# A modelled SBUF port in the kernel's own scheduler, ELU sums on VectorE, and a longer look-ahead

## The chip, the cores and the metric

One core of a Trainium2 chip runs the whole program. The metric is the device time in microseconds of one execution; the median of three runs of the kernel before is 866.75 us. The engines are TensorE (PE in the profile, its weight loads PEld), VectorE (DVE), ScalarE (ACT), GpSimd (POOL) and SyncE (SP), which here issues nearly all DMAs from one in-order queue.

## The reference

Local attention with two kinds of mask, followed by an ELU feed-forward layer, all in float32:

```python
# q, k, v: (8, 8, 576, 64); w_in: (512, 2048); w_out: (2048, 512)
scores = (q @ k.transpose(0, 1, 3, 2)) / sqrt(64)
rel = pos[:, None] - pos[None, :]
mask_plain = (rel >= 0) & (rel < 32)                          # heads 0 to 3
mask_dil = (rel >= 0) & (rel < 128) & (rel % 4 == 0)          # heads 4 to 7
scores = where(mask, scores, -1e9)
attn = exp(scores - scores.max(-1)); attn /= attn.sum(-1) + 1e-9
x = (attn @ v), heads side by side                            # (4608, 512)
h = x @ w_in
g = where(h > 0, h, exp(min(h, 0)) - 1)
out = g @ w_out                                               # (4608, 512)
```

## The kernel before

The 4608 tokens are nine chunks of 512. The first three ("plain chunks", c = 0, 1, 2) are computed directly: for each of 16 blocks f of the hidden dimension, a first product into a PSUM bank `h`, an ELU (ScalarE exp and relu, VectorE `stt!`), a split of the result into a rounded high part and a remainder ("cast" on ScalarE, "rest" on VectorE, since three single-pass products of high and low parts replace one float32 product), and a second product into `o_ps` for block f - 2. The other six chunks are taken two at a time as three "wide" chunks (`wide_chunk`, w = 0, 1, 2), with a Strassen-like scheme of seven products instead of eight in both matrix products: 28 "in" steps and 28 "out" steps of 12 matmuls each. Their weight combinations (names like S1, A22) are computed once on chip from the weights, stored in DRAM (`combined`, `plain_out`, `sums_out`) and loaded again into a ring of four places (`load_combined`, L950 to L965): the load for step i + 3 can go out when step i - 1 has freed its place. Each "in" step is followed by additions and ELU pieces on VectorE and ScalarE (`behind_inner`). Each "out" step needs an operand "unit" (`make_unit`, L1162): the difference of two ELU blocks (`summed`, for four of the seven names), a cast on ScalarE, a rest on VectorE. At the turn from "in" to "out", units are prepared up to LEAD = 4 ahead in the first wide chunk and up to 7 in the others (L1182). When all four steps of an output are done, `stored` adds two PSUM banks to a copy (`gh`, `x` or `e`, VectorE) and stores to `out_t`; the first of these outputs is C11, written from `gh`.

Attention of the batches b = 2 to 7 runs as side work between these steps, pair of heads by pair: scores on TensorE into the banks `a_ps`, masks added by VectorE into a tile `sm`, then `pair_steps` ("max", "less", "exp", "sum", "more", "over", "times", six copies "placed" into `pt`, and a transpose "turned"), then the product with v. Further side work is the sums of weights for the Strassen scheme ("sums", POOL) and the splits of some weights ("late").

The order of instructions on each engine is fixed by the program's order (`inorder`). That order comes from a small scheduler in the kernel itself: `clock` holds a modelled time for each engine, `Ordered` wraps an engine and advances its clock by a linear cost, `work(until)` emits the side steps that start earliest by these clocks until they would end after `until`, `better` may move a step named in SHARED from its engine to POOL, and `freer` gives a step to VectorE or POOL, whichever ends first by the model. `output_ready` and `scores_ready` decide when TensorE takes a piece of attention. An `Ordered` VectorE writes a tensor_tensor as a scalar_tensor_tensor (L611), except where it reads PSUM (`from_bank`). L614 is the line through which nearly all ordered steps of VectorE, ScalarE and POOL pass, and L607 that of the additions from PSUM; L147 is that of all matmuls.

Of the kernel before, what the change touches and what calls it, by code (L numbers as in the profile page):

```python
# [71 lines left out]
STORE_LAG = 1  # L72
FILL = 3.5
WIDE_STEP = 4.0
# [20 lines left out]
def body(ctx: ExitStack, tc: tile.TileContext, q, k, v, masks, w_in, w_out, out, out_t):  # L95
# [240 lines left out]
    def start_sum(half):  # L336
# [205 lines left out]
    def masks_added(hp, places, sm, eng=nc.vector):  # L542

        dil = hp >= NPAIR // 2
        for i in range(max(len(p) for p in places)):
            for h in range(2):
                n0, n1, s_ps = places[h][i]
                add = eng.from_bank if isinstance(eng, Ordered) else eng.tensor_tensor
                last = add(out=sm[:, h * NU + n0:h * NU + n1, :].rearrange("p n j -> p (n j)"), in0=s_ps[:QB, :(n1 - n0) * 2 * G],
                                        in1=mask_sb[:, int(dil), n0 * 2 * G:n1 * 2 * G], op=ALU.add)  # L550
        return last
# [24 lines left out]
    def probabilities(b, hp, sm, nmx, sums):  # L576
# [13 lines left out]
        return b, hp, tr  # L590

    class Ordered:

# [5 lines left out]

        def cost(self, kw, name=None):  # L600
            if self.name == "POOL" and name in ("copy", "tensor_copy"):
# [3 lines left out]
        def from_bank(self, **kw):  # L605
            clock[self.name] = self.free() + self.cost(kw)
            return inorder(self.eng.tensor_tensor(**kw))  # L607

        def __getattr__(self, name):
            def emit(**kw):  # L610
                if self.name == "DVE" and name == "tensor_tensor":  # L611
                    return self.scalar_tensor_tensor(out=kw["out"], in0=kw["in0"], scalar=1.0, in1=kw["in1"], op0=ALU.mult, op1=kw["op"])
                clock[self.name] = self.free() + self.cost(kw, name)
                return inorder(getattr(self.eng, name)(**kw))  # L614
            return emit

    vec, act, pool = Ordered(nc.vector, "DVE", 0.155, 0.00104), Ordered(nc.scalar, "ACT", 0.19, 0.00083), Ordered(nc.gpsimd, "POOL", 0.45, 0.00185)
# [6 lines left out]
    finished, at = {}, {}  # L624
    phase, late_until, second_done = [0], [2], {}

    def emit_next(pair):

        name, eng, op, kw, *more = better(pair.pop(0), finished.get(id(pair), 0.0))
        clock[eng.name] = max(eng.free(), finished.get(id(pair), 0.0), floor(name))  # L630
        ins = getattr(eng, op)(**(kw() if callable(kw) else kw))
        finished[id(pair)] = clock[eng.name] + LATENCY
# [11 lines left out]
    def better(step, since):  # L644

        name, eng, op, kw, *more = step
        if name[0] not in SHARED or not phase[0] < SHARED_UNTIL:
            return step
        other = [name, pool, {"copy": "tensor_copy"}.get(op, op), kw, *more]
        return min(step, other, key=lambda x: max(x[1].free(), since) + cost(x))  # L650

    def work(until):

        while True:
            side[:] = [pair for pair in side if pair]
            starts = []
            for n, pair in enumerate(side):
                key = pair[0][0]
                if ready_for(key):
                    step = better(pair[0], finished.get(id(pair), 0.0))  # L660
                    start = max(step[1].free(), finished.get(id(pair), 0.0), floor(key))
                    if start + cost(step) <= until:
                        starts.append((start, 0 if key[0][-1] == "!" else 1 if key[0][:4] == "late" else 3 if key[0] == "sums" else 2, n))
            if not starts:
                return
            emit_next(side[min(starts)[-1]])
# [27 lines left out]

    sms, kept = [], []

    def other_sm(*at):
        del sms[1:]
        if at:
            sms.append([at[0].rearrange("p o t -> p (o t)")[:QB, :2 * NU * 2 * G].rearrange("p (u j) -> p u j", u=2 * NU), None])  # L700

    def own_steps(c, f, h_ps):
# [35 lines left out]

    def pair_steps(b, hp, sm):
# [5 lines left out]
        yield ("max", b, hp), vec, "tensor_reduce", dict(out=mx, in_=sm, op=ALU.max, axis=mybir.AxisListType.X)  # L745
        yield ("less", b, hp), vec, "tensor_tensor", dict(out=sm, in0=sm, in1=wide(mx), op=ALU.subtract)
        yield ("exp", b, hp), act, "activation", dict(out=sm, in_=sm, func=AF.Exp, scale=0.125)
# [17 lines left out]
    def one_scores(b, hp):  # L765
# [3 lines left out]
        i = b * NPAIR + hp  # L769
        scores(s_ps, *qk_of.pop(i), True)  # L770
        clock["now"] = clock["PE"]
        room = free_sms()[0]
        sm, room[1] = room[0], (b, hp)
        masks_added(hp, [[(0, NU, a)] for a in s_ps], sm, vec)
        banks_free[0] = clock["DVE"] + LATENCY
        side.append([list(x) for x in pair_steps(b, hp, sm)])
        kept_lists.append(side[-1])
        finished[id(side[-1])] = clock["DVE"]
        load_qk(i + 2)
        landed["qk", i + 2] = clock["PE"] + LANDING  # L780

    def one_output(b, hp):
# [11 lines left out]
        if (b, hp) == (CS + 1, NPAIR - 1):  # L794
            kept.append(sms[-1][0])
            other_sm(slots("a-1'", 0, 1))
        load_v(i + 2)
        landed["v", i + 2] = clock["PE"] + LANDING

    def output_ready():  # L800
# [4 lines left out]
        if phase[0] < HOME[b]:  # L805
            return False
        return max(at["turned", b, hp] + LATENCY, landed.get(("v", b * NPAIR + hp), 0.0), banks_free[0]) <= clock["PE"] + (TOLERANCE if phase[0] > 2 else EARLY)

    def scores_ready():
# [7 lines left out]
        last = ("placed", *rooms[0][1], GU - 1, 1) if rooms[0][1] else None  # L817
        return max(at.get(last, 0.0), landed.get(("qk", b * NPAIR + hp), 0.0), banks_free[0]) <= clock["PE"] + (TOLERANCE if phase[0] > 2 else EARLY)

# [181 lines left out]
    def wide_operand(w, what):  # L1001
# [7 lines left out]
        if do == "make":  # L1009
            for r0, r1, (left, right) in wide_stretches(w, 0, 1):  # L1010
                x0, x1 = {"T1": lambda: (right(0), left(0)), "T2": lambda: (right(1), temporary(w, "T1")[:, :, r0:r1]), "T3": lambda: (right(1), right(0)),
                          "T4": lambda: (left(1), temporary(w, "T2")[:, :, r0:r1])}[name]()
                freer(t[:, :, r0:r1]).tensor_tensor(out=t[:, :, r0:r1], in0=x0, in1=x1, op=ALU.subtract)
        elif t is not None:
# [11 lines left out]
    def wide_chunk(w):  # L1026
# [52 lines left out]
        def added(to, tos, key):  # L1079
            for i in range(2):  # L1080
                vec.from_bank(out=to[i], in0=tos[i], in1=us[key][i], op=ALU.add)

# [70 lines left out]
        def summed(k):  # L1153

            if k < len(over):
# [29 lines left out]
        def stored(name, tos, key):  # L1185

            for r in range(2):
# [3 lines left out]
                for i in range(n):  # L1191
                    cols = slice(i * TC // n, (i + 1) * TC // n)
                    vec.from_bank(out=o[:, cols], in0=tos[r][:, cols], in1=us[key][r][:, cols], op=ALU.add)
                    def write(o=o, t=t, s=s, cols=cols):
# [380 lines left out]
```

## Time and profile before

| | us |
|---|---|
| median of 3 runs (lowest, highest) | 866.75 (865.43, 866.88) |
| the profiled execution | 864.79 |
| its span, first to last instruction | 863.0 |
| TensorE busy | 825.8 |
| VectorE busy | 650.9 |
| ScalarE busy | 519.7 |
| POOL busy | 286.9 |

The mean granted TensorE clock is 0.988. The "busy" of TensorE includes matmuls that run slowly; the rows of a single group (n matmuls in so many us) tell the pace. Rows of the timeline give the start, the length, the engine, the line, the operation, output<-inputs, the shape and the count; in brackets stand the idle time of the engine before the row and what ended it. The time of a VectorE or POOL row runs from its issue to its end, so that it includes time in which it is held up.

### The profile page before, as it was taken

The numbers are of one execution on the slowest core, as the hardware profiler recorded it, in microseconds if no ns is written. First come the engines' busy times: TensorE is split into PE (matmuls) and PEld (weight loads), VectorE is DVE, ScalarE is ACT, GpSimd is POOL, SyncE is SP. The second block draws the span as 40 slices with busy tenths as digits, with TensorE's granted clock in tenths as the row PEclk, the third lists the DMA queues.
The fourth block names the chain that finished last, engine by engine and source line by source line (L and its number), as shares of the span: only waits on it lengthen the run. The fifth ranks groups of instructions, "written<-read, shape, count | busy, mean of one in ns | idle before, by whom it ended". The sixth has DMA issues, their size and how long they took to land.

```text
span 863.0 us, 16083 instructions
## 1 busy us (share of the span) xinstructions
PE 825.8 (96%) x6304; PEld 651.5 (75%) x6304; DVE 650.9 (75%) x758; ACT 519.7 (60%) x873; POOL 286.9 (33%) x250
## 2 busy tenths in 40 slices
PE   6999999999999999899998899999996999999798
PEld 4566888778878778678776678788885888888686
DVE  6999996987757758478979895577799654467972
ACT  5889776665555546668855353688753436676340
POOL 3000001464676666686651722002062020023400
PEclk9999999999999999999999999999998999999999
DMA  8999878646465894899876659766644686666555
GB/s 302 379 384 372 258 225 278 196 159 197 132 216 184 247 283 139 319 373 335 290 254 181 210 169 311 226 181 189 186 154 156 194 264 194 194 193 194 165 178 168
DMA packets 105322, 199.13 MB, mean 231 GB/s; under 512 B 13120, under 2 KB 58528, under 8 KB 104992
## 3 DMA queue, kind: packets, MB, share of 16 engines
q1 hardware_dynamic: 105104, 197.81, 70.8%
q8 instruction: 49, 0.80, 0.4%
q10 hardware_dynamic: 144, 0.31, 0.1%
q14 instruction: 25, 0.20, 0.1%
HBM read 148.54 MB, written 49.55 MB: 230 GB/s over the span
## 4 chain that ended last, share of the span: by engine, by line
PE 76%; DVE 12%; DMA 5%; ACT 4%; issue 2%; SPq 0%; DVEq 0%; POOL 0%; ACTq 0%
PE o_ps L147 39%; PE h L147 24%; PE a_ps L147 13%; DVE a L614 5%; DVE r L614 4%; ACT x L614 1%; DMA outputs<-a-1_3413 1%; DMA r<-sums_out 1%; DMA r<-combined 1%; DMA r<-w_in 1%; DMA vt<-v 1%; ACT a L614 1%; DVE a-1_3413 L607 0%; DMA qt<-q 0%; DVE a-1_3413 L614 0%
## 5 line engine op out<-in xcount | busy, mean ns | idle before, releaser
L147 PE MATMUL o_ps<-a,r 128*128 128x512 f32 x792 | 188.7, 392 | 4.6 <-DVE a L614 4.6
L147 PEld LDWEIGHTS o_ps<-a,r 128*128 128x128 f32 x792 | 147.5, 188 | 37.6 <-DVE a L614 5.8
L147 PE MATMUL o_ps<-r,r 128*128 128x512 f32 x432 | 109.7, 405 | 15.7 <-DMA r<-sums_out 11.8
L147 PEld LDWEIGHTS o_ps<-r,r 128*128 128x128 f32 x432 | 84.0, 196 | 36.6 <-issue 12.6
L614 POOL TENSOR_TENSOR a<-a 128x256 f32<-128x256 f32 (+1 forms) x59 | 59.3, 1009 | 126.0 <-DVE r L614 116.6
L147 PE MATMUL h<-a,r 128*128 128x512 f32 x396 | 94.3, 390 | 0.0
L147 PEld LDWEIGHTS h<-a,r 128*128 128x128 f32 x396 | 74.0, 188 | 15.9
L147 PE MATMUL h<-x,r 128*128 128x512 f32 x324 | 79.7, 395 | 0.0
L147 PE MATMUL o_ps<-a,gh 128*128 128x512 f32 x216 | 76.1, 449 | 0.0
L147 PEld LDWEIGHTS h<-x,r 128*128 128x128 f32 x324 | 60.1, 188 | 13.8 <-DVE a L188 0.2
L147 PE MATMUL a_ps<-a,r 128*128 128x512 f32 x252 | 60.2, 391 | 3.0 <-DVE a L614 1.5
L614 ACT ACTIVATE x<-x 128x1024 f32<-128x1024 f32 (+1 forms) x53 | 54.9, 1041 | 8.3 <-POOL x L614 7.6
L147 PEld LDWEIGHTS a_ps<-a,r 128*128 128x128 f32 x252 | 46.9, 188 | 14.7 <-DVE a L614 2.8
L614 DVE SCALAR_TENSOR_TENSOR a<-a,a 128x1024 fp32r<-128x1024 f32 (+2 forms) x32 | 47.6, 1492 | 7.7 <-ACT a L614 7.3
L614 DVE SCALAR_TENSOR_TENSOR a<-r,a 128x1024 fp32r<-128x1024 f32 x30 | 45.7, 1530 | 10.0 <-ACT a L614 10.0
L147 PEld LDWEIGHTS o_ps<-a,gh 128*128 128x128 f32 x216 | 39.7, 188 | 17.8 <-issue 10.5
L614 ACT CAST a<-r 128x1024 fp32r<-128x1024 f32 x30 | 31.3, 1047 | 34.5 <-DVE r L614 27.1
L614 POOL TENSOR_TENSOR sm<-sm,nmx 96x768 f32<-96x768 f32 x4 | 5.9, 1472 | 126.4 <-DMA out<-e 121.1
L614 ACT CAST a<-a 128x1024 fp32r<-128x1024 f32 (+1 forms) x30 | 28.9, 962 | 29.6 <-DVE a L614 18.3
L147 PE MATMUL o_ps<-r,gh 128*128 128x512 f32 x136 | 42.7, 395 | 0.0
L614 ACT COPY e<-o_ps 128x512 f32<-128x512 f32 x44 | 24.8, 587 | 28.2 <-PE o_ps L147 24.8
L614 DVE SCALAR_TENSOR_TENSOR gl<-e,gh 128x512 fp32r<-128x512 f32 x34 | 28.1, 827 | 17.7 <-ACT gh L614 14.0
(235 smaller groups left out, 1662.0 us busy)
## 6 DMA issues: line engine op xcount, KB each, us to landing
r<-combined SPq DMA_DIRECT2D x84, 512.0 KB, 4.5
r<-sums_out SPq DMA_DIRECT2D x48, 512.0 KB, 4.6
r<-plain_out SPq DMA_DIRECT2D x36, 512.0 KB, 4.2
vt<-v SPq DMA_DIRECT2D x30, 384.0 KB, 4.8
kt<-k SPq DMA_DIRECT2D x29, 304.0 KB, 4.7
qt<-q SPq DMA_DIRECT2D x30, 288.0 KB, 4.2
r<-w_in SPq DMA_DIRECT2D x16, 512.0 KB, 6.8
r<-w_out SPq DMA_DIRECT2D x16, 512.0 KB, 7.2
```

The costliest lines, as they stand in the source:

```text
L147: return inorder(nc.tensor.matmul(to, w, x, **kw))
L614: return inorder(getattr(self.eng, name)(**kw))
```

## The change

- `summed` (the ELU block differences of the "out" operands) always goes to VectorE (SUMMED_BY = "vec"); before, `freer` chose VectorE or POOL. The T differences of `wide_operand` still go through `freer` (MADE_BY = "both").
- The modelled clocks get a shared port: `Ordered.start` lets a VectorE or POOL step with two SBUF inputs (LOCKING) begin only after the other engine's modelled step, and a POOL step pushes VectorE's clock on by the overlap. `better` counts a POOL step double (PORT_COST).
- SHARED shrinks to "placed": "less", "times" and "late" are no longer offered to POOL. Consecutive "placed" copies may start together.
- VectorE's tensor_tensor is issued as such, and the "more" step becomes a tensor_scalar.
- Look-ahead: FILL from 3.5 to 5.5 (how far past TensorE side work is emitted in the plain chunks), LEAD from 4 to 6, BACKLOG from 5 to 8 (how far VectorE may be behind when new scores are taken), EARLY from -1 to 0. The modelled costs of POOL steps are changed too.
- Switches that are off (MASKED_BY_PE, EXP_BY_UNIT empty) or set as before (SUMS_BY = "pool") change nothing.

The core of the diff:

```diff
-FILL = 3.5
+FILL = 5.5
-EARLY = -1.0
+EARLY = 0.0
-LEAD = 4
-BACKLOG = 5.0
-SHARED, SHARED_UNTIL = ("placed", "less", "times", "late"), 3.5
+LEAD = 6
+BACKLOG = 8.0
+LOCKING = {"DVE": ("tensor_tensor", "scalar_tensor_tensor", "tensor_scalar", "tensor_copy"), "POOL": ("tensor_tensor", "tensor_copy", "copy")}
+SHARED = ("placed",)
+PORT_COST = 1.0
...
             if self.name == "POOL" and name in ("copy", "tensor_copy"):
-                return 0.3 + 0.0009 * (kw if isinstance(kw, int) else length(kw["out"]))
+                return 0.35 + 0.00053 * (kw if isinstance(kw, int) else length(kw["out"]))
...
+        def start(self, name, kw, since=0.0):
+            t = max(self.free(), since)
+            if self.locks(name, kw):
+                for a, b in port[PORT_WITH[self.name]]:
+                    if a <= t < b:
+                        t = b
+                        if self.name == "POOL":
+                            break
+            return t
...
             def emit(**kw):
-                if self.name == "DVE" and name == "tensor_tensor":
-                    return self.scalar_tensor_tensor(out=kw["out"], in0=kw["in0"], scalar=1.0, in1=kw["in1"], op0=ALU.mult, op1=kw["op"])
-                clock[self.name] = self.free() + self.cost(kw, name)
+                t = self.start(name, kw)
+                clock[self.name] = t + self.cost(kw, name)
+                if self.locks(name, kw):
+                    port[self.name] = port[self.name][-7:] + [(t, clock[self.name])]
+                    if self.name == "POOL":
+                        clock["DVE"] += sum(max(0.0, min(b, clock["POOL"]) - max(a, t)) for a, b in port["DVE"])
...
-    ... pool = ... Ordered(nc.gpsimd, "POOL", 0.45, 0.00185)
+    ... pool = ... Ordered(nc.gpsimd, "POOL", 0.19, 0.00212)
...
-        return min((vec, pool), key=lambda eng: eng.free() + eng.cost(length(out)))
+        return min((vec, pool), key=lambda eng: eng.start("tensor_tensor", 0) + eng.cost(length(out)))
...
-        yield ("more", b, hp), vec, "scalar_tensor_tensor", dict(out=sums, in0=sums, scalar=1e-9, in1=sums, op0=ALU.add, op1=ALU.max)
+        yield ("more", b, hp), vec, "tensor_scalar", dict(out=sums, in0=sums, scalar1=1e-9, scalar2=None, op0=ALU.add)
...
-                    freer(to).tensor_tensor(out=to, in0=x, in1=y, op=ALU.subtract)
+                    (freer(to) if SUMMED_BY == "both" and w == 0 else vec).tensor_tensor(out=to, in0=x, in1=y, op=ALU.subtract)
```

More of the change, by code (lines that the diff above doesn't have):

```diff
@@ L80 @@
 TOLERANCE = 0.0
-EARLY = -1.0
+EARLY = 0.0
 HOME = {2: 1, 3: 2, 4: 2.4, 5: 3.2, 6: 3.2, 7: 4.2}
 START = 1.0
-LEAD = 4
-BACKLOG = 5.0
-SHARED, SHARED_UNTIL = ("placed", "less", "times", "late"), 3.5
-SUMS_FROM = 7
+LEAD = 6
+BACKLOG = 8.0
+LOCKING = {"DVE": ("tensor_tensor", "scalar_tensor_tensor", "tensor_scalar", "tensor_copy"), "POOL": ("tensor_tensor", "tensor_copy", "copy")}
+PORT_WITH = {"DVE": "POOL", "POOL": "DVE"}
+SHARED = ("placed",)
+SHARED_UNTIL = 3.5
+SUMS_FROM = 7
+PORT_COST = 1.0
+SUM_COST = 0.0
+SUM_DELAY = 0.0
+SUMMED_BY = "vec"
+MADE_BY = "both"
+SUMS_BY = "pool"
+MASKED_BY_PE = ()
+EXP_BY_UNIT = ()
 LATE_AT = 2, 4, 5, 7, 9, 11, 12
@@ L363, in start_sum, with banks_after @@
         kept_lists.append(steps)
+    bank_user = [None]
+    def banks_after():
+        return banks_free[0] if not bank_user[0] else at.get(bank_user[0], 1e9) + LATENCY
     x32 = {}
@@ L547, in masks_added @@
                 n0, n1, s_ps = places[h][i]
-                add = eng.from_bank if isinstance(eng, Ordered) else eng.tensor_tensor
-                last = add(out=sm[:, h * NU + n0:h * NU + n1, :].rearrange("p n j -> p (n j)"), in0=s_ps[:QB, :(n1 - n0) * 2 * G],
+                last = eng.tensor_tensor(out=sm[:, h * NU + n0:h * NU + n1, :].rearrange("p n j -> p (n j)"), in0=s_ps[:QB, :(n1 - n0) * 2 * G],
                                         in1=mask_sb[:, int(dil), n0 * 2 * G:n1 * 2 * G], op=ALU.add)
@@ L590, in probabilities @@
         return b, hp, tr
+    port = {"DVE": [], "POOL": []}
     class Ordered:
@@ L600, in cost, with locks @@
         def cost(self, kw, name=None):
+            if self.name == "ACT" and isinstance(kw, dict) and length(kw["out"]) <= 2 * G:
+                return 0.33
             if self.name == "POOL" and name in ("copy", "tensor_copy"):
-                return 0.3 + 0.0009 * (kw if isinstance(kw, int) else length(kw["out"]))
+                return 0.35 + 0.00053 * (kw if isinstance(kw, int) else length(kw["out"]))
             return self.fixed + self.each * (kw if isinstance(kw, int) else max(length(kw[n]) for n in ("out", "in_", "in0") if n in kw))
-        def from_bank(self, **kw):
-            clock[self.name] = self.free() + self.cost(kw)
-            return inorder(self.eng.tensor_tensor(**kw))
+        def locks(self, name, kw):
+            if self.name == "ACT" or name not in LOCKING[self.name]:
+                return False
+            return not isinstance(kw, dict) or all(kw[n].space != bass.MemoryType.PSUM for n in ("in_", "in0", "in1") if n in kw)
@@ L631, in emit_next @@
         ins = getattr(eng, op)(**(kw() if callable(kw) else kw))
-        finished[id(pair)] = clock[eng.name] + LATENCY
+        ends_at[id(pair)] = max(ends_at.get(id(pair), 0.0), clock[eng.name])
+        if not pair or pair[0][0][0] != name[0] or name[0] not in ("exps", "placed"):
+            finished[id(pair)] = ends_at.pop(id(pair)) + LATENCY
         passed.add(name)
@@ L646, in better, with begins @@
         name, eng, op, kw, *more = step
[L647 to L650, printed above, removed]
+        others = []
+        if name[0] in SHARED and phase[0] < SHARED_UNTIL:
+            others.append([name, pool, {"copy": "tensor_copy"}.get(op, op), kw, *more])
+        if name[0] == "sums":
+            other = [name, vec, op, kw, *more] if op == "tensor_tensor" else [name, act, "copy", kw, *more]
+            if SUMS_BY == "vec":
+                return other
+            if SUMS_BY == "both":
+                others.append(other)
+        return min([step, *others], key=lambda x: begins(x, since) + cost(x) * (1 + PORT_COST if x[1] is pool else 1) + (SUM_COST if x[0][0] == "sums" and x[1] is not pool else 0))
+    def begins(step, since):
+        return step[1].start("no lock" if step[0][0] == "stt!" else step[2], step[4] if callable(step[3]) else step[3], since)
     def work(until):
@@ L660, in work @@
                     step = better(pair[0], finished.get(id(pair), 0.0))
-                    start = max(step[1].free(), finished.get(id(pair), 0.0), floor(key))
+                    start = begins(step, max(finished.get(id(pair), 0.0), floor(key)))
                     if start + cost(step) <= until:
-                        starts.append((start, 0 if key[0][-1] == "!" else 1 if key[0][:4] == "late" else 3 if key[0] == "sums" else 2, n))
+                        starts.append((start + (SUM_DELAY if key[0] == "sums" else 0.0), 0 if key[0][-1] == "!" else 1 if key[0][:4] == "late" else 3 if key[0] == "sums" else 2, n))
             if not starts:
@@ L769, in one_scores @@
         i = b * NPAIR + hp
-        scores(s_ps, *qk_of.pop(i), True)
+        if b in MASKED_BY_PE:
+            for a in s_ps:
+                mm(a[:QB, :NU * 2 * G], ones_sb, mask_sb[:, int(hp >= NPAIR // 2), :], start=True, stop=False)
+        scores([a[:QB, :NU * 2 * G] for a in s_ps], *qk_of.pop(i), b not in MASKED_BY_PE)
         clock["now"] = clock["PE"]
@@ L773, in one_scores @@
         sm, room[1] = room[0], (b, hp)
-        masks_added(hp, [[(0, NU, a)] for a in s_ps], sm, vec)
-        banks_free[0] = clock["DVE"] + LATENCY
-        side.append([list(x) for x in pair_steps(b, hp, sm)])
+        if b in MASKED_BY_PE:
+            bank_user[0] = ("exps", b, hp, 2 * NU - 1)
+            side.append([list(x) for x in pair_steps(b, hp, sm, s_ps)])
+            finished[id(side[-1])] = clock["PE"] + LATENCY
+        else:
+            masks_added(hp, [[(0, NU, a)] for a in s_ps], sm, vec)
+            banks_free[0] = clock["DVE"] + LATENCY
+            side.append([list(x) for x in pair_steps(b, hp, sm)])
+            finished[id(side[-1])] = clock["DVE"]
         kept_lists.append(side[-1])
-        finished[id(side[-1])] = clock["DVE"]
         load_qk(i + 2)
@@ L796, in one_output @@
             other_sm(slots("a-1'", 0, 1))
+            sm_from[0] = clock["PE"] + LANDING
         load_v(i + 2)
@@ L817, in scores_ready @@
         last = ("placed", *rooms[0][1], GU - 1, 1) if rooms[0][1] else None
-        return max(at.get(last, 0.0), landed.get(("qk", b * NPAIR + hp), 0.0), banks_free[0]) <= clock["PE"] + (TOLERANCE if phase[0] > 2 else EARLY)
+        return max(at.get(last, 0.0) if last else sm_from[0], landed.get(("qk", b * NPAIR + hp), 0.0), banks_after()) <= clock["PE"] + (TOLERANCE if phase[0] > 2 else EARLY)
     def pieces():
@@ L1080, in added @@
             for i in range(2):
-                vec.from_bank(out=to[i], in0=tos[i], in1=us[key][i], op=ALU.add)
+                vec.tensor_tensor(out=to[i], in0=tos[i], in1=us[key][i], op=ALU.add)
         es = {}
@@ L1192, in stored @@
                     cols = slice(i * TC // n, (i + 1) * TC // n)
-                    vec.from_bank(out=o[:, cols], in0=tos[r][:, cols], in1=us[key][r][:, cols], op=ALU.add)
+                    vec.tensor_tensor(out=o[:, cols], in0=tos[r][:, cols], in1=us[key][r][:, cols], op=ALU.add)
                     def write(o=o, t=t, s=s, cols=cols):
```

32 lines of the change are left out of this document (23 added, 9 removed).

## The prediction

> **What bounds the kernel now.** I read the page's first part and the clock first, then a table by stages, then who made TensorE wait, then the order of time around the two longest waits.
>
> ```profile
> span 863.0 us, 16083 instructions
> PE 825.8 (96%) x6304; PEld 651.5 (75%) x6304; DVE 650.9 (75%) x758; ACT 519.7 (60%) x873; POOL 286.9 (33%) x250
> ```
>
> TensorE is busy 825.8 of 863.0 us, so about 37 us are idle. The stages after the start, which the change leaves alone, show where (columns: stage, its length, busy us with counts of PE, PEld, DVE, ACT, POOL, granted clock, DMA share, GB/s):
>
> ```profile
> 212.00:324.00 112.00, 111.39 (x1170) 88.66 (x1169) 75.39 (x105) 59.84 (x114) 76.26 (x88) 1.00 0.66 205
> 348.00:470.00 122.00, 114.54 (x1038) 90.03 (x1036) 95.28 (x105) 83.65 (x122) 72.47 (x67) 0.99 0.87 299
> 470.00:502.00 32.00, 27.20 (x122) 21.21 (x116) 28.25 (x20) 11.90 (x16) 22.52 (x9) 1.00 0.64 202
> 627.40:662.00 34.60, 27.52 (x114) 21.71 (x113) 34.60 (x21) 14.26 (x17) 19.72 (x6) 0.91 0.50 160
> 662.00:788.60 126.60, 126.60 (x558) 104.74 (x558) 72.58 (x80) 74.62 (x94) 10.72 (x6) 1.00 0.67 203
> 788.60:824.00 35.40, 30.34 (x125) 24.31 (x124) 35.40 (x24) 14.94 (x16) 16.65 (x5) 0.90 0.53 171
> ```
>
> The stage from 662 to 788 has no idle TensorE at all. The holes are at 348 to 502 (first wide chunk), 627 to 662 (second) and 788 to 824 (third), where each wide chunk turns from its "in" to its "out" products. In the last two stages VectorE is busy for the whole stage (34.60 of 34.60, 35.40 of 35.40) and the clock falls to 0.91 and 0.90. The list of waits names transfers (us in total, times, longest):
>
> ```profile
> PE o_ps L147 <- DMA r<-sums_out: 11.8, 2, 6.8
> PE a_ps L147 <- DMA r<-combined: 1.5, 1, 1.5
> ```
>
> But the sums_out load is only last in a line. In order of time on VectorE, POOL, the SyncE queue and TensorE around 800 us:
>
> ```profile
> 789.74 3.43 DVE L614 SCALAR_TENSOR_TENSOR r<-a,r 128x1024 fp32r<-128x1024 f32 x1
> 793.09 1.21 DVE L614 SCALAR_TENSOR_TENSOR a<-a,a 128x1024 fp32r<-128x1024 f32 x1
> 794.22 1.21 DVE L614 SCALAR_TENSOR_TENSOR r<-r 128x1024 f32<-128x1024 f32 x1
> 812.15 1.27 DVE L607 TENSOR_TENSOR gh<-o_ps,hh 128x512 f32<-128x512 f32 x2
> ```
> ```profile
> 788.76 3.32 POOL L614 TENSOR_TENSOR a-1_3413<-a-1_3413 128x1024 f32<-128x1024 f32 x1 [21.38 <-DVE a-1_3413 L614]
> ```
> ```profile
> 797.29 5.76 SPq L964 DMA_DIRECT2D r<-sums_out  x3
> 812.85 0.94 SPq L1195 DMA_DIRECT2D out_t<-gh  x2
> 813.88 0.91 SPq L964 DMA_DIRECT2D r<-sums_out  x2
> ```
> ```profile
> 797.10 11.04 PE L147 MATMUL h<-a,r 128*128 128x512 f32 x48
> 818.95 4.91 PE L147 MATMUL o_ps<-r,r 128*128 128x512 f32 x12 [5.00 <-DMA r<-sums_out]
> ```
>
> VectorE alone starts one such step every 1.13 us (793.09 to 794.22); next to a POOL sum it takes 3.43. So VectorE reaches the C11 additions (gh<-o_ps,hh) at 812.15, though TensorE had ended their products and begun the next (bank h) at 797.10. The two stores of gh stand in SyncE's queue ahead of the next weight load, which goes out at 813.88 and lands at about 818.8. TensorE waits 5.00 us, and then its clock is low: 12 matmuls in 4.91 us where 2.7 is normal.
>
> **The change part by part.** *Sums of ELU blocks move from POOL to VectorE* (`summed`, L1153). These are POOL's 128x1024 plain-f32 steps:
>
> ```profile
> L614 POOL TENSOR_TENSOR r<-r 128x1024 f32<-128x1024 f32 x9 | 26.4, 2943 | 18.2 <-DVE a L614 18.1
> L614 POOL TENSOR_TENSOR a<-a,a 128x1024 f32<-128x1024 f32 x5 | 16.7, 3348 | 4.6 <-DVE a L614 4.6
> L614 POOL TENSOR_TENSOR a-1_3413<-a,a-1_3413 128x1024 f32<-128x1024 f32 x4 | 12.5, 3136 | 15.1 <-DVE a L614 15.1
> L614 POOL TENSOR_TENSOR a<-a 128x1024 f32<-128x1024 f32 x3 | 7.9, 2623 | 116.7 <-DVE r L614 116.6
> L614 POOL TENSOR_TENSOR a-1_3413<-a-1_3413 128x1024 f32<-128x1024 f32 x2 | 6.6, 3324 | 44.7 <-DVE a-1_3413 L614 44.7
> ```
>
> That is 23, or 23 x 1.13 = 26 us more for VectorE. Where it has idle time (72.58 busy of 126.60 in the stage before) this costs nothing; that idle time is the cover. Where it is full, it trades: each POOL sum now holds a VectorE step up by 3.43 - 1.21 = 2.2 us, and on VectorE it would take 1.13. The two stretches up to the C11 additions:
>
> ```profile
> 627.40:652.80 25.40, 25.03 (x108) 19.69 (x106) 25.40 (x12) 11.23 (x14) 19.72 (x6) 1.00 0.39 122
> 788.60:812.10 23.50, 23.44 (x104) 19.11 (x103) 23.50 (x12) 10.75 (x12) 16.65 (x5) 1.00 0.47 145
> ```
>
> The count of 12 on VectorE takes in the step that ends as the stretch begins, so 11 steps; with POOL's 5 sums they are 16 x 1.13 = 18.1 us. The additions then start at 788.6 + 18.1 = 806.7 instead of 812.15, end 1.27 later, and the load goes out at about 808.5, landing 4.93 later (813.88 to 818.8 now) at 813.4. TensorE needs it at 813.9 (818.95 - 5.00). The margin is half a microsecond. In the second chunk: 627.4 + 18.1 = 645.5, load out at 647.3, landing at 652.1 (4.77 for that load), needed at 652.6; but there POOL's sixth step, a T difference of the next chunk, can still hold VectorE up by some 2 us.
>
> What is there to win:
>
> ```profile
> 654.61 4.77 DMA r<-sums_out
> 659.52 7.17 PE o_ps L147 x24
> 813.88 4.93 DMA r<-sums_out
> 818.95 7.64 PE o_ps L147 x24
> 837.47 21.77 PE o_ps L147 x96
> ```
>
> 24 matmuls take 21.77/4 = 5.44 us at full clock. Second chunk: 6.8 wait + 1.7 slow = 8.5, of which I take 7.5. Third: 5.0 + 2.2 = 7.2, of which I take 6.5. A remainder of one or two would not cool the clock, as the first chunk shows:
>
> ```profile
> 456.62 0.50 PE L147 MATMUL o_ps<-r,r 128*128 128x512 f32 x1 [1.52 <-ACT r L614]
> 458.08 4.26 PE L147 MATMUL o_ps<-r,r 128*128 128x512 f32 x11 [0.96 <-DVE r L614]
> 490.14 2.79 PE L147 MATMUL o_ps<-a,r 128*128 128x512 f32 x11 [3.27 <-DVE a L614]
> ```
>
> After 3.27 us idle, 11 matmuls took 2.79, near the 2.5 of full clock; after short waits in a row they took 4.26, so a remainder may cost up to 1.8 more, and by that end the sum below would be 2 x 1.8 = 3.6 worse. I take the single wait's row, which is what a late load makes. [...]
>
> *First wide chunk.* Late part (470 to 502): 4.8 us idle, from VectorE steps of 3.4 us beside POOL's sums, five of which go; I take 3.5 (bounds 0 and 4.8), since POOL may keep the T differences there. Early part (450 to 458): of the 7.5 us idle in the stage 348 to 470, the two waits quoted are 2.5, and 1.8 of slow clock follow. There operands were prepared 4 ahead; with LEAD 6, nearer to the 7 of the later chunks, which have no such wait, some fit earlier: I take 3 (bounds 0 and 5.5, with what idle time the combined loads leave). The price of LEAD 6 is two more units, 2 x 2 x 1.13 = 4.5 us, ahead of the C11 additions; the third chunk as worked out bears 806.7 - 797.1 = 9.6 us between TensorE and these additions, so I cost it at nothing.
>
> *The order by a modelled lock; FILL 5.5, EARLY 0, BACKLOG 8; POOL offered only "placed".* The softmax's "less" and "times" and the "late" weight splits go back to VectorE: even if POOL took all "less" and "times" of the 24 pairs now, 48 steps shorter than 1.21 us over three stages, and VectorE has 36 idle us of 112 in the one shown: cover. The "placed" copies, 384 wide and so under the 0.6 us that 512 take below, lean to ScalarE, which idles 52 of 112 there: cover again, and each would cost TensorE its 0.5 or so if that were gone. TensorE has 0.6 us to win in that stage, so this part can hardly gain, only lose. The ELU chain and the matmuls around it:
>
> ```profile
> L614 ACT ACTIVATE e<-h 128x512 f32<-128x512 f32 x34 | 20.3, 597 | 18.7 <-PE h L147 17.1 <-DMA out<-e 1.5
> L614 ACT ACTIVATE e<-e 128x512 f32<-128x512 f32 x34 | 21.5, 632 | 0.7
> L614 DVE SCALAR_TENSOR_TENSOR e<-h,e 128x512 f32<-128x512 f32 x34 | 23.2, 683 | 5.4 <-ACT e L614 4.2 <-issue 1.2
> ```
>
> The h bank is reused after three blocks of 12 matmuls, 8.2 us; exp, relu and stt take 1.9; looking 5.5 ahead instead of 3.5 lets other work stand before them up to 5.5 - 2.7 = 2.8 us. That leaves 3.5. I take +1 (bounds 0 and +8). SyncE's order of loads shifts too, and with it the wait for a combined load (1.5 in the list): I take -1 (bounds -3, the rest of that stage's idle time, and +4, half a load's landing late twice).
>
> *VectorE's tensor_tensor is issued as such, not as scalar_tensor_tensor.*
>
> ```profile
> L614 DVE SCALAR_TENSOR_TENSOR gl<-e,gh x34: 650/692/2366, 126.0 to 340.0; 128x512 fp32r<-128x512 f32 x34
> L905 DVE TENSOR_TENSOR gl<-e,gh x7: 676/684/696, 79.7 to 120.9; 128x512 fp32r<-128x512 f32 x7
> ```
>
> Alone they cost the same (692 and 684 ns). Beside POOL the new form is not shown; between no wait and the old 2.2 I take the old, the same operands. [...] A form that never waited would take the T difference's 2 us off as well. "more" as tensor_scalar: 24 steps of 12 elements, nothing.
>
> Sum: -7.5 - 6.5 - 3.5 - 3 + 1 - 1 = -20.5. The profiled execution took 864.79 us, 1.96 under the median of 866.75, so 844.3 for its like, and **846.3 us** for the median.
>
> **The rivals.** *Only the two late holes go*, and new order elsewhere gives back what the first chunk gains: 866.75 - 14 + 2 = 855. For it: nothing to win in the plain chunks. *The C11 additions stay late*: the margins are 0.5 us; if VectorE is 3 us later than worked out (T differences, casts late), half of the two late holes stays, (8.5 + 7.2)/2 = 7.9, and with 3 for the rest as it is the time is 866.75 - 7.9 + 3 = 862. *Nothing changes*, gains and losses level: 867. *Slower*: the longer look-ahead puts attention work before ELU, and TensorE waits at its h bank. It decides when ELU is over 3.5 us later than modelled; at 4.3 in each of 32 blocks that is 0.8 x 32 = 26 us, so about 872. Against it: the plain chunks' gl steps (row above) keep to their 692 ns in the median, with single ones at 2366.
>
> **How the numbers follow.** The two late holes rest on rows alone and give 14 us; only their margin is thin, so what leaves at least half of them stands together at 0.87: forecast 0.62 (838 to 853), only the late holes 0.18, additions late 0.07, no change 0.04, slower 0.09. Runs agree within about 0.2%, so faster 0.87, same 0.04, slower 0.09. All bounds on the good side give 866.75 - 8.5 - 7.2 - 4.8 - 5.5 - 3 = 837.8; the second rival is taken in with some room: 837 to 861.
>
> **What would show it.** POOL without 128x1024 f32 sums after 440 us, VectorE steps of 1.2 us throughout 627 to 650 and 788 to 807 of the old time; C11 additions within 10 us of TensorE's last A12 product; no wait of TensorE on sums_out over 2 us and a clock near 1.00. Wrong: if sums_out waits remain, or if waits on "gh" or "gl", or of the h matmuls, appear before 340 us.

## The result and the profile after

The changed kernel takes 833.94 us (median, 832.92 to 835.20), the kernel before 866.09 us beside it: a ratio of 0.963, 95% interval 0.9612 to 0.9648, or 32 us less. The prediction was 846.3 (837 to 861): the direction was right, the time lies 3 us below the range. The profiled execution took 835.20 us with a span of 833.0 (before: 864.79 and 863.0), so the traces have 30.0 us of the difference to explain.

First the page's head of the kernel after, then a table by stages (same columns as before: stage, length, busy us of PE, PEld, DVE, ACT, POOL, granted clock, DMA share, GB/s), then, from the list of what TensorE waited for (us in total, times, longest), its first line and two short waits for transfers:

```profile
span 833.0 us, 16070 instructions
PE 819.3 (98%) x6304; PEld 649.9 (78%) x6304; DVE 650.3 (78%) x788; ACT 524.0 (63%) x879; POOL 229.4 (28%) x214
```
```profile
212.00:324.00 112.00, 111.38 (x1237) 88.35 (x1236) 82.06 (x116) 64.01 (x120) 73.67 (x83) 1.00 0.74 232
348.00:470.00 122.00, 121.45 (x944) 97.19 (x943) 102.29 (x115) 86.14 (x126) 43.62 (x45) 1.00 0.85 275
470.00:502.00 32.00, 32.00 (x142) 26.48 (x142) 29.87 (x28) 16.74 (x19) 22.22 (x2) 1.00 0.66 212
605.00:640.00 35.00, 35.00 (x173) 28.52 (x173) 31.36 (x29) 21.42 (x26) 12.61 (x1) 1.00 0.59 183
766.10:800.00 33.90, 33.90 (x151) 28.07 (x150) 33.90 (x32) 16.10 (x17) 0.00 (x0) 1.00 0.67 209
```
```profile
PE a L158 <- DMA masks_sb<-masks: 4.1, 1, 4.1
PE a_ps L158 <- DMA vt<-v: 0.6, 1, 0.6
PE a_ps L158 <- DMA r<-combined: 0.5, 1, 0.5
```

The turns of all three wide chunks (470 to 502, 605 to 640, 766 to 800) now run without an idle microsecond of TensorE at full clock, and sums_out is gone from the list. VectorE is as busy as before (650.3), although it does more: in these stretches nearly all its 128x1024 steps take 1.22 us, where those beside POOL's sums took up to 3.43 before. In order of time in the third chunk, on VectorE, the SyncE queue and TensorE:

```profile
766.13 1.22 DVE L653 TENSOR_TENSOR r<-r,r 128x1024 fp32r<-128x1024 f32 x1
...
784.30 1.22 DVE L653 TENSOR_TENSOR r<-r,r 128x1024 fp32r<-128x1024 f32 x1
785.43 1.28 DVE L653 TENSOR_TENSOR gh<-o_ps,hh 128x512 f32<-128x512 f32 x2
```
```profile
766.66 19.36 SPq L1035 DMA_DIRECT2D r<-sums_out  x8
786.14 0.35 SPq L1266 DMA_DIRECT2D out_t<-gh  x1
788.42 0.32 SPq L1035 DMA_DIRECT2D r<-plain_out  x1
788.79 0.42 SPq L1266 DMA_DIRECT2D out_t<-gh  x1
```
```profile
774.63 11.04 PE L158 MATMUL h<-a,r 128*128 128x512 f32 x48
788.23 5.60 PE L158 MATMUL o_ps<-r,r 128*128 128x512 f32 x24
```

Two things changed. From 766.13 to 784.30 VectorE does 17 steps of 1.22 us, and the C11 additions come 785.43 - 774.63 = 10.8 us behind their products (before: 15.05). And the two stores of gh, which stood behind six of the eight sums_out loads, now stand behind all eight. Nothing in the diff says so: the kernel pins the order of its compute steps (`inorder`) but not that of its DMAs, and when the sums moved, the place that the framework gave the stores moved too. The second change was not in the prediction.

To compare kernels by stage I add up, over all matmuls, by how much the time from one matmul's start to the next one's exceeds the median for its kind in the kernel after. That counts idle time and slow clock together. It falls from 103.0 to 73.1 us, 29.9 of the 30.0 us of span:

| us lost by TensorE | to 320 | 320-360 | 360-440 | 440-520 | 520-625 | 625-700 | 760 on | all |
|---|---|---|---|---|---|---|---|---|
| before | 54.0 | 3.0 | 9.1 | 14.3 | 5.6 | 9.4 | 7.6 | 103.0 |
| after | 54.9 | 1.6 | 7.7 | 2.1 | 6.8 | 0.0 | 0.0 | 73.1 |
| b_store | 53.8 | 2.7 | 8.9 | 14.3 | 5.6 | 2.0 | 0.4 | 87.7 |
| a_store | 57.0 | 0.8 | 7.5 | 2.0 | 6.9 | 4.9 | 1.3 | 80.5 |
| b_sums | 53.4 | 2.9 | 9.2 | 9.5 | 5.8 | 0.0 | 0.0 | 80.7 |
| b_sums_lead6 | 55.0 | 3.5 | 9.0 | 6.2 | 9.5 | 0.8 | 0.0 | 84.1 |
| b_sums_lead6_look | 56.2 | 8.8 | 8.2 | 6.8 | 5.6 | 0.0 | 0.0 | 85.6 |
| a_lead4 | 55.1 | 1.5 | 7.6 | 5.2 | 9.2 | 0.0 | 0.0 | 78.6 |
| a_noport | 56.0 | 10.5 | 8.2 | 12.8 | 5.6 | 0.0 | 0.0 | 93.2 |
| a_short | 54.3 | 8.8 | 6.7 | 2.3 | 7.0 | 0.0 | 0.0 | 79.2 |
| a_poolw0 | 54.8 | 0.5 | 7.6 | 14.6 | 7.0 | 0.0 | 0.0 | 84.5 |
| a_freersums | 55.0 | 2.1 | 7.8 | 14.0 | 9.9 | 10.5 | 8.2 | 107.5 |
| a_freersums_store | 54.4 | 1.1 | 7.6 | 14.5 | 8.8 | 6.4 | 3.1 | 100.0 |

The other rows are the experiments; names with b_ are edits of the kernel before, with a_ of the kernel after. Between 700 and 760 us, which has no column, only a_freersums_store loses anything (4.1 us).

### The profile page after: what moved, and what is told of

Same layout as the page of the kernel before. It is cut to its first block, busy times and chain, and to the rows that moved or that the text cites. A ratio compares the mean times of both kernels' runs of the same rounds, so it can differ in the third digit from the quotient of the medians.

```text
span 833.0 us, 16070 instructions
## 1 busy us (share of the span) xinstructions
PE 819.3 (98%) x6304; PEld 649.9 (78%) x6304; DVE 650.3 (78%) x788; ACT 524.0 (63%) x879; POOL 229.4 (28%) x214
## 4 chain that ended last, share of the span: by engine, by line
PE 96%; DMA 2%; ACT 1%; issue 0%; SPq 0%; DVE 0%; DVEq 0%; ACTq 0%
PE o_ps L158 50%; PE h L158 30%; PE a_ps L158 14%; DMA r<-combined 1%; DMA vt<-v 1%; PE b L158 1%; ACT pt L554 1%; DMA qt<-q 0%; PE c L158 0%; PE d L158 0%; PE a L158 0%; ACT a L653 0%; ACT e L653 0%; DVE x L653 0%; ACT a-1_3448 L653 0%
## 5 line engine op out<-in xcount | busy, mean ns | idle before, releaser
L158 PE MATMUL o_ps<-r,r 128*128 128x512 f32 x432 | 103.4, 390 | 0.0
L158 PEld LDWEIGHTS o_ps<-r,r 128*128 128x128 f32 x432 | 80.8, 188 | 17.7 <-DVE r L653 0.7
L653 POOL TENSOR_TENSOR a<-a 128x256 f32<-128x256 f32 x64 | 58.3, 914 | 26.8 <-ACT x L653 10.1
L653 POOL COPY pt<-sm 32x384 f32<-32x384 f32 x23 | 15.6, 679 | 168.5 <-DVE sm L653 159.4
L653 POOL TENSOR_TENSOR x<-x,x 128x640 f32<-128x640 f32 (+3 forms) x9 | 26.1, 2910 | 105.1 <-ACT x L653 68.0
L158 PEld LDWEIGHTS o_ps<-a,gh 128*128 128x128 f32 x216 | 39.7, 188 | 17.9 <-issue 10.5
L653 DVE TENSOR_TENSOR a<-a,a 128x1024 fp32r<-128x1024 f32 (+2 forms) x39 | 47.7, 1228 | 5.8 <-ACT a L653 5.6
L653 DVE SCALAR_TENSOR_TENSOR e<-h,e 128x512 f32<-128x512 f32 x34 | 23.2, 682 | 24.1 <-ACT e L653 23.2
L653 DVE TENSOR_TENSOR a<-r,a 128x1024 fp32r<-128x1024 f32 x30 | 36.6, 1225 | 6.3 <-ACT a L653 6.3
```

The lines of the kernel that those rows point to most:

```text
L158: return inorder(nc.tensor.matmul(to, w, x, **kw))
```

## The experiments

**The stores alone (b_store).** Only SyncE's queue changes.

```diff
-            nc.sync.dma_start(out=to, in_=src)                  # load_combined
+            loads.append(nc.sync.dma_start(out=to, in_=src).ins)
...
-                        nc.sync.dma_start(out=out_t[...], in_=o[:, cols])
+                        with tc.issue_after(loads[-1]) if name == "C11" and w else ExitStack(): nc.sync.dma_start(out=out_t[...], in_=o[:, cols])
...
-                        later.append((STORE_LAG, write))
+                        later.append((4 if name == "C11" and w else STORE_LAG, write))
```

> The kernel before, with the two stores of C11 in the second and third wide chunk placed two loads further back in SyncE's queue; no engine's order changes, VectorE and POOL do the same steps. Theory A (queue order: TensorE waited only because the stores, which wait for late additions, stood ahead of its loads): both waits on sums_out and the slow clock behind them go, 8.5 + 7.2 = 15.7 us, so 850 us (848 to 853), although the additions still come about 15 us after their products. Theory B (VectorE's lateness itself holds TensorE, through banks or operands): the waits return under another name and the time stays at 862 to 866 us.

850.84 us (849.34 to 856.15), ratio 0.9838 [0.9809, 0.9866]. Its VectorE, SyncE queue and TensorE around 800 us:

```profile
796.09 3.43 DVE L614 SCALAR_TENSOR_TENSOR a<-a,a 128x1024 fp32r<-128x1024 f32 x1
803.92 1.28 DVE L607 TENSOR_TENSOR gh<-o_ps,hh 128x512 f32<-128x512 f32 x2
```
```profile
804.63 0.94 SPq L1195 DMA_DIRECT2D out_t<-gh  x2
805.66 5.83 SPq L964 DMA_DIRECT2D r<-plain_out  x4
```
```profile
802.46 5.96 PE L147 MATMUL o_ps<-r,r 128*128 128x512 f32 x24
```

VectorE's steps still take 3.43 us beside POOL, yet the S2 products run through (24 in 5.96 us): late additions hurt TensorE only through the stores in front of its loads. Of the two late holes 17.0 - 2.4 = 14.6 us go, with two stores moved in each of the two chunks. Theory A holds.

**Fast VectorE, stores in the old place (a_store).** The loads from the seventh sums_out load on are held behind the stores; no engine but SyncE changes.

```diff
-            nc.sync.dma_start(out=to, in_=src)
+            with tc.issue_after(held[max(x for x in held if x <= i)]) if min(held, default=999) <= i < 999 else ExitStack(): nc.sync.dma_start(out=to, in_=src)
...
-                        nc.sync.dma_start(out=out_t[...], in_=o[:, cols])
+                        held[loaded[0] + 1 if name == "C11" and w else 999] = nc.sync.dma_start(out=out_t[...], in_=o[:, cols]).ins
```

> The kernel after, with these two stores put back to where they stood before, directly ahead of the third load of the S2 products; nothing else moves. Theory A with fast VectorE (as the prediction took it): the additions start 10.6 us behind their products in the third chunk, the load goes out about 13.5 us and lands about 18.5 us behind them, needed at about 16.8: a wait on sums_out of 1 to 2.5 us in each of the two chunks, with a slow clock of up to 1.8 us behind each: 836 to 842 us. Rival (the order of the queue is worth all of the 15.7 us of the two late holes): 846 us or more. Rival (it no longer matters): 833 to 835 us.

840.33 us (839.19 to 842.92), ratio 0.971 [0.9688, 0.9732], 6.4 us above the changed kernel. TensorE, VectorE and the queue in the second chunk, then TensorE in the third:

```profile
623.93 11.04 PE L158 MATMUL h<-a,r 128*128 128x512 f32 x48
643.41 4.57 PE L158 MATMUL o_ps<-r,r 128*128 128x512 f32 x12 [3.00 <-DMA r<-sums_out]
```
```profile
636.60 1.29 DVE L653 TENSOR_TENSOR gh<-o_ps,hh 128x512 f32<-128x512 f32 x2
```
```profile
638.35 0.92 SPq L1035 DMA_DIRECT2D r<-sums_out  x2
```
```profile
798.65 3.00 PE L158 MATMUL o_ps<-r,r 128*128 128x512 f32 x12 [1.02 <-DMA r<-sums_out]
```

This is the case that the prediction worked out. The additions come 12.7 us behind their products in the second chunk (636.60 - 623.93), the stores stand behind six sums_out loads, the wait is 3.00 us and 12 matmuls take 4.57 us after it; in the third chunk the wait is 1.02 us. With the stores in the old place, fast VectorE leaves 4.9 + 1.3 = 6.2 us of the late holes (table). The expectation's total was right, its even split was not.

**The sums alone (b_sums).**

```diff
-                    freer(to).tensor_tensor(out=to, in0=x, in1=y, op=ALU.subtract)
+                    vec.tensor_tensor(out=to, in0=x, in1=y, op=ALU.subtract)
```

> The kernel before, with all sums of ELU blocks on VectorE and nothing else edited. Theory 1 (the lock between POOL's sums and VectorE is the cause): both late holes go (15.7 us) and 4 to 8 us of the late part of the first wide chunk: 842 to 847 us. Theory 2 (the gain comes from the new order by the modelled lock and the longer look-ahead): 858 us or more. Theory 3 (it comes from the plain form of VectorE's subtraction): 862 us or more.

843.01 us (841.96 to 844.22), ratio 0.9738 [0.9718, 0.9757]: 22.9 of the 32 us. Both late holes are gone. Here too the stores moved behind all eight loads by themselves (third chunk: eight loads from 774.17, the first store at 793.66), so this run does not part the faster VectorE from the new queue; b_store and a_store do. Theory 1 holds for the larger part; 9 us remain for the rest of the change.

**LEAD.** In the old order (b_sums_lead6, `LEAD = 6` added to b_sums) and taken back in the new one (a_lead4, `LEAD = 4`):

> The same with LEAD 6 besides, still without the modelled lock, the look-ahead and the new form. Theory 1: another 3 to 5 us, from the first wide chunk around 340 to 460 us: 837 to 843 us, so that the rest of the change is worth 3 to 9. Theory 2: still 854 us or more. Rival on LEAD: no difference to the kernel without it, within 1 us.

> The kernel after with LEAD 4 again. As predicted (LEAD 6 takes the waits on late operands at 450 to 458 us away): they return, 836 to 839 us. Rival, after the run in which LEAD 6 without the rest of the new order made the kernel 3 us slower: LEAD is not what gains, 832 to 835 us.

b_sums_lead6 took 846.01 us (844.0 to 847.38), ratio 0.9769 [0.9747, 0.9792], 3.0 more than without: it wins 3.3 us at 440 to 520 and loses 3.7 at 520 to 625 and 1.6 before 320. Its expectation missed. a_lead4 took 838.69 us (837.34 to 840.34), ratio 0.9682 [0.9659, 0.9704], 4.8 above the changed kernel: 3.1 at 440 to 520 and 2.4 at 520 to 625. So the same constant costs 3 us in one order and gains 5 in the other. LEAD 7 (a_lead7) changes nothing more: 833.84 us (832.43 to 834.97), ratio 0.962 [0.9598, 0.9643].

> The kernel after with LEAD 7, as many operands ahead in the first wide chunk as in the later two. If LEAD 6 gained by early operands and some waits are left at 440 to 560 us: 831 to 833 us. If the extra unit delays the C11 additions or the attention work of the first chunk instead: 835 us or more. No difference: 833 to 835 us.

**The lock in the model and the look-ahead.** The look-ahead without the lock: on b_sums_lead6 (`FILL = 5.5`, `EARLY = 0.0`, `BACKLOG = 8.0`); and the changed kernel with `locks` returning False (a_noport). The lock with part of the look-ahead taken back, FILL and EARLY half the way: the changed kernel with `FILL = 4.5`, `EARLY = -0.5`, `BACKLOG = 5.0` (a_short) and with `BACKLOG = 5.0` alone (a_backlog). The lock with FILL and EARLY all the way back was not run.

```diff
         def locks(self, name, kw):
 
+            return False
```

> The kernel before with the sums on VectorE, LEAD 6 and the longer look-ahead (FILL 5.5, EARLY 0, BACKLOG 8), still without the modelled lock. Without the look-ahead it took 846 us. Theory (looking further ahead helps only where the planner knows the lock; without it VectorE is later than planned and ELU late for TensorE): 850 to 860 us, lost between 200 and 360 us and at 460 us, as in the changed kernel without the modelled lock. Rival (the look-ahead is what brings the changed kernel from 846 to 834): 834 to 840 us.

> The kernel after with the modelled lock switched off: the planner never holds VectorE's and POOL's steps apart; sums on VectorE, LEAD 6, the longer look-ahead and the new form stay. Theory (the 9 us by which the changed kernel beats the one with the sums alone come from the modelled lock): 840 to 844 us, with VectorE steps of over 2 us beside POOL in the plain chunks and the first wide chunk. Rival (they come from the look-ahead and LEAD together): 833 to 836 us.

> The kernel after with a shorter look-ahead: FILL 4.5, EARLY -0.5, BACKLOG 5; the modelled lock, LEAD 6 and the sums on VectorE stay. Theory (the modelled lock carries the gain and the look-ahead little): 833 to 837 us. Rival (without the longer look-ahead the operands of the first wide chunk are late again): 839 us or more, with waits at 440 to 560 us.

> The kernel after with BACKLOG 5 alone, so that new scores wait while VectorE has over 5 us of work before it. If only the limit on the work ahead of VectorE matters in the look-ahead: as the kernel with all three shortened. If it does not: 833 to 835 us.

| kernel | us (lowest to highest) | ratio [interval] |
|---|---|---|
| b_sums_lead6_look | 849.66 (848.0 to 851.6) | 0.9807 [0.9783, 0.9831] |
| a_noport | 858.52 (855.79 to 860.43) | 0.991 [0.9888, 0.9932] |
| a_short | 840.15 (839.68 to 840.51) | 0.9696 [0.9676, 0.9717] |
| a_backlog | 833.35 (833.09 to 833.88) | 0.9619 [0.9599, 0.9639] |

The look-ahead does not pay without the lock: in the old order it costs 3.7 us (849.66 against 846.01), and without the modelled lock the changed kernel loses 24.6 us, far more than the 9 in question; of the 20.1 us that its trace shows, the table puts 8.9 at 320 to 360 and 10.7 at 440 to 520. With the lock but the shorter look-ahead 6.2 us are lost; the kernel is then still 2.9 us faster than b_sums. The table puts 7.2 us of loss in one place, 320 to 360, and 1.0 of gain behind it. In that kernel, on VectorE and on TensorE:

```profile
335.76 0.67 DVE L653 TENSOR_TENSOR a<-a-1_3431,a 128x512 f32<-128x512 f32 x1
337.59 1.23 DVE L653 TENSOR_TENSOR a<-a,a 128x1024 fp32r<-128x1024 f32 x1 [1.17 <-ACT a L653]
338.74 1.29 DVE L653 TENSOR_TENSOR gl<-e,gh 128x512 fp32r<-128x512 f32 x2
```
```profile
339.48 0.79 PE L158 MATMUL o_ps<-r,gl 128*128 128x512 f32 x1 [4.93 <-DVE gl L653]
```

The first operand of the wide chunk (337.59) stands ahead of the last ELU blocks' gl, waits for a ScalarE cast, and TensorE waits 4.93 us for gl. The changed kernel, with the longer look-ahead, has the same step in the same place, and it waits even longer:

```profile
337.71 1.49 DVE L653 TENSOR_TENSOR a<-a,a 128x1024 fp32r<-128x1024 f32 x1 [1.43 <-ACT a L653]
340.07 2.25 DVE L653 TENSOR_TENSOR gl<-e,gh 128x512 fp32r<-128x512 f32 x2
```
```profile
337.60 2.88 PE L158 MATMUL a_ps<-r,r 128*128 128x512 f32 x12
```

There TensorE is still at earlier blocks until 337.6 and then has 12 matmuls of the wide chunk to do, so gl comes in time. So the 6 us of the look-ahead are a matter of how the two engines' orders fit at the end of the plain chunks, not a gain spread over them. BACKLOG alone is worth nothing. Not tested one by one are the narrower SHARED, the changed costs in the model and the "placed" copies that start together. They are, with forms that cost nothing (next run), what parts a_noport from b_sums_lead6_look: without the lock, this rest makes the kernel 8.9 us slower (858.52 against 849.66).

**The form (a_stt).** VectorE's subtractions of two SBUF inputs as scalar_tensor_tensor again, the order unchanged.

```diff
+                if self.name == "DVE" and name == "tensor_tensor" and all(kw[n].space != bass.MemoryType.PSUM for n in ("in0", "in1")):
+                    real, kv = "scalar_tensor_tensor", dict(out=kw["out"], in0=kw["in0"], scalar=1.0, in1=kw["in1"], op0=ALU.mult, op1=kw["op"])
```

> The kernel after with VectorE's subtractions of two SBUF inputs issued as scalar_tensor_tensor again; the order is the same. As predicted (the form costs nothing alone and locks the same way): 833 to 836 us. Rival (the plain form does not wait for POOL and carries the 9 us): 840 to 844 us, with steps of 3.4 us beside POOL's that the changed kernel does not have.

834.29 us (833.86 to 835.19), ratio 0.9631 [0.9609, 0.9653]: no difference, as predicted.

**Sums back on POOL.** All of them (a_freersums, `freer(to)` in `summed`); those of the first wide chunk alone (a_poolw0, `SUMMED_BY = "both"`); all of them with the stores late (a_freersums_store, the edit of b_store besides).

> The kernel after with the sums of ELU blocks given to whichever of VectorE and POOL its model has free first, which with the modelled lock sends all 48 of them to POOL (before: 23, after: none). Theory (POOL's sums hold VectorE up and so the operands of the first wide chunk and the C11 additions): the waits of the first wide chunk return and, where the stores stand early in SyncE's queue, those on sums_out: 848 to 862 us, above the 843 of the kernel before with the sums alone moved. Rival (the new order and the later stores hide the lock): 834 to 838 us.

> The kernel after with the 16 sums of ELU blocks of the first wide chunk offered to POOL again, which takes all of them under the modelled lock; the second and third chunk keep them on VectorE. If the first wide chunk gained from the sums only what was predicted (3.5 us): 836 to 839 us. If the lock set all of its late operands, with the slow clock behind the waits (12.2 us between 440 and 520 us in the trace): 843 to 848 us, lost between 440 and 520 us and nowhere after 600 us.

> The kernel with all 48 sums on POOL (867 us) with the two stores of C11 of the second and third chunk placed two loads further back, as in the run on the kernel before. If the waits on sums_out came from the stores' place alone: they go, 17 to 18 us less, 848 to 851 us, though VectorE is held up by 15 or 16 POOL sums in each chunk. If VectorE is now too late for TensorE's operands as well: some of it stays under another name, 853 to 862 us.

a_freersums took 867.08 us (864.52 to 869.65), ratio 1.0002 [0.9989, 1.0016]: with the sums on POOL the whole gain is gone, more than expected, and the stores stand behind six loads again. a_poolw0 took 846.18 us (844.96 to 847.68), ratio 0.9764 [0.9744, 0.9783]: 12.2 us more than the changed kernel, all of it (14.6 against 2.1) between 440 and 520. Its first chunk has 16 sums on POOL, where the kernel before has 9. VectorE, the queue and TensorE there:

```profile
465.09 3.42 DVE L653 TENSOR_TENSOR a<-a,a 128x1024 fp32r<-128x1024 f32 x1
468.42 3.41 DVE L653 TENSOR_TENSOR r<-r,r 128x1024 fp32r<-128x1024 f32 x1
471.75 1.28 DVE L653 TENSOR_TENSOR gh<-o_ps,hh 128x512 f32<-128x512 f32 x2
```
```profile
472.46 0.95 SPq L1266 DMA_DIRECT2D out_t<-gh  x2
473.50 1.87 SPq L1035 DMA_DIRECT2D r<-sums_out  x4
```
```profile
453.00 5.06 PE L158 MATMUL o_ps<-r,r 128*128 128x512 f32 x11 [2.73 <-DVE r L653]
462.55 11.04 PE L158 MATMUL h<-a,r 128*128 128x512 f32 x48
478.39 4.18 PE L158 MATMUL o_ps<-a,r 128*128 128x512 f32 x9 [4.80 <-DMA r<-sums_out]
```

The plain form takes 3.41 us beside POOL, as the old one did (3.43). An operand is late (2.73 us, and 11 matmuls in 5.06 behind it, where 2.5 is normal), and then the queue of the late holes appears in the first chunk too: additions, stores, loads, a wait of 4.80 us. The additions come 471.75 - 462.55 = 9.2 us behind their products, hardly later than in the changed kernel (467.50 - 458.50 = 9.0). What differs is again the stores' place: here behind four sums_out loads, in the changed kernel behind seven.

a_freersums_store took 862.22 us (859.08 to 863.14), ratio 0.9944 [0.9926, 0.9962]: only 4.9 us of the expected 17. Waits on sums_out are gone from its list. But of the two late holes' 18.7 us 9.5 stay, and 4.1 come back between 700 and 760, as the second theory said. Behind the stores of the second chunk, TensorE gets its operands at the pace of VectorE beside POOL, a step every 3.34 us:

```profile
661.11 3.01 PE L158 MATMUL a_ps<-a,r 128*128 128x512 f32 x12 [0.21 <-DVE a L653]
664.44 3.04 PE L158 MATMUL a_ps<-a,r 128*128 128x512 f32 x12 [0.32 <-DVE a L653]
```

Twelve matmuls take 3.33 us from start to start here, where 2.72 is normal; ScalarE's copies and casts, which stand behind POOL's sums, make TensorE wait too (1.0 us at 674.94, 2.3 at 705.02). So with all 16 sums of a chunk on POOL, TensorE's operands themselves are late, and the stores' place is not enough. It was enough in b_store, where five of POOL's sums stand ahead of the additions.

## Why the prediction was right, and where it was wrong

*The cause* was right: POOL's sums hold VectorE's steps for 2.2 us each, the C11 additions come late, their stores stand in SyncE's queue ahead of the loads. b_store, b_sums and a_freersums show each link.

*The step that failed most* is the one on the order by a modelled lock and the longer look-ahead, "so this part can hardly gain, only lose", taken at +1 with -1 for the combined loads. It looked for a gain in the plain chunks alone. The terms for the sums and LEAD (-20.5 together) came out near in their total: b_sums_lead6 is 19.9 us faster than the kernel before. By the table it has 16.2 us less in the late holes and 8.1 less at 440 to 520, but 3.9 more at 520 to 625, where LEAD's price had been put at nothing. The other 12.1 us, down to 833.94, come with the lock, the look-ahead and the rest of the new order, which the sum put at nothing; of the 11.0 that the traces show of them, 4.1 lie at 440 to 520, 2.7 at 520 to 625, 1.9 at 320 to 360 and 1.3 at 360 to 440. The parts lean on each other, so this is one way of sharing them out: without the lock the changed kernel loses 24.6 us. How much of the 12.1 belongs to the lock alone stays open.

*The late holes* (-14 taken, -17.0 measured) came out near, but partly by luck, since the step failed that said "The margin is half a microsecond" with the stores where they stood. In the third chunk its lag of 9.6 us was 10.8: 17 steps stand ahead of the additions, not 16 (785.43 - 766.13 = 19.3 us, not 18.1), for a sum that POOL did earlier in the kernel before (at 764.97) now falls into the stretch. In the second chunk the lag was 12.7 us: there TensorE's products besides start 6.6 us after VectorE's first step (622.29 - 615.67), where they started 7.9 after it (635.34 - 627.39). LEAD has no part in this; it acts on the first wide chunk alone. So the prediction's own sign, additions within 10 us of the products, did not come about. a_store shows that this alone would have left 6.2 us, against the 1.7 that I left. What took the rest away is that the stores' place changed with the sums, which I had taken as fixed: two errors of opposite sign.

*The first wide chunk* (-3.5 and -3, together -6.5) was mis-sized; between 440 and 520 us it is -12.2, with the lock's share above in it. I took parts of the waits read off the rows and counted slow clock behind the early ones only; from 440 to 502 before, TensorE was busy 53.41 of 62.00 us at a clock of 0.97,

```profile
440.00:502.00 62.00, 53.41 (x325) 41.29 (x324) 52.64 (x41) 33.63 (x47) 34.58 (x16) 0.97 0.64 198
```

which is 8.6 us of idle time and 0.03 x 62 = 1.9 of slow clock, where I took 6.5. a_poolw0 gives POOL's sums 12.2 us here, with more of them on POOL than before, and a_lead4 gives LEAD 3.1 (and 2.4 behind 520): they overlap, so the two prices do not add up.

*The range's low end* was built from the same bounds (837.8), so it shared the gap: 1.3 us of the late holes (17.0 against 15.7) and 1.9 of the first chunk (12.2 against 10.3) were outside them. That this brings 837.8 close to the measured 833.94 is partly chance: the combined loads gave 1.4 us of the 3 in the low end, and 520 to 625 us, which had no term, cost 1.2.

*The plain chunks* (+1): -0.5 up to 360 us, inside what repeats; *combined loads* (-1): -1.4 at 360 to 440. The rival "only the two late holes" (855) did not happen, though b_sums, with 4.8 us more, is near it in kind. The rival by which the longer look-ahead makes ELU late is real where the lock is not modelled: TensorE waits 4.6 us for gl at 351.65 in b_sums_lead6_look and 4.4 for gh at 351.00 in a_noport. It is not a matter of a long look-ahead alone, since a_short, with a shorter one, waits 4.9; in the changed kernel no such wait appears. *The form*: right, no difference.

## What to carry to other kernels

When a load is last in a chain of waits, look at what stands ahead of it in its queue: moving two stores by two places, in two chunks, was worth 15 us with no engine any faster, and the queue's order can move with an edit of another engine's steps; it is not a constant of the prediction. When you size a hole, count idle time and the slow clock behind it by one sum over the matmuls. And do not give each constant of a planner a price of its own, nor put a new order at nothing because one stage has no idle time: LEAD cost 3 us in one order and gained 5 in another, and the look-ahead cost 3.7 without the lock.

## What the runs showed of the hardware

VectorE and POOL side by side were slower here than VectorE alone. With all sums on POOL (a_freersums_store), their steps ended in turn:

```profile
640.97 3.42 DVE L653 TENSOR_TENSOR a<-a-1_3448,a 128x1024 fp32r<-128x1024 f32 x1
644.31 3.41 DVE L653 TENSOR_TENSOR a<-a,a 128x1024 fp32r<-128x1024 f32 x1
```
```profile
646.60 3.37 POOL L653 TENSOR_TENSOR a-1_3448<-a,a-1_3448 128x1024 f32<-128x1024 f32 x1
649.92 3.38 POOL L653 TENSOR_TENSOR a<-a,a 128x1024 f32<-128x1024 f32 x1
```

One VectorE and one POOL step every 3.34 us, where VectorE does both in 2 x 1.13 = 2.27. Beside an unbroken chain on VectorE it was the POOL step that took long. In the kernel after:

```profile
624.43 12.61 POOL L653 TENSOR_TENSOR x<-x,x 128x896 f32<-128x896 f32 x1 [37.02 <-issue]
```
```profile
634.97 1.28 DVE L653 TENSOR_TENSOR gh<-o_ps,hh 128x512 f32<-128x512 f32 x2
636.17 1.95 DVE L653 TENSOR_TENSOR a<-a,a 128x1024 f32<-128x1024 f32 x1
```

The T difference takes 12.61 us, where one of the same shape took 2.13 (583.88), and ends at 637.04, just behind the additions that read o_ps, while every VectorE step with two SBUF inputs before them takes 1.22; only the next one is held, by 0.7 us, where I had feared 2. A POOL step of 128x256 in the first wide chunk took 19.71 us in the same way (470.10 to 489.81), where one with two inputs of that shape took 0.73 elsewhere. Which of the two began first did not tell here which is held: the VectorE step before POOL's began first (623.62), but those from 624.75 on began behind POOL's 624.43 and ended ahead of it all the same. Why the steps ended in turn in one case and not in the other, no run here shows.

The pace of the matmuls behind a wait did not go by the length of that wait: 12 took 4.57 us after 3.00 us idle (a_store) and 11 took 5.06 after 2.73 (a_poolw0), but in the kernel before 11 took 2.79 after 3.27, at a granted clock of 1.00 (490.14 to 492.93), and 11 took 4.26 after 0.96, at 0.63 (458.08 to 462.34). So the one row that the prediction took for a remainder (2.79 us) was no measure for the wait in a_store; what else sets the clock, no run here shows.
